# Moving two thirds of the transposes of g from TensorE to the DMA engines in a fused RWKV and MoE kernel

## The chip, the cores and the metric

The kernel runs on one core of a Trainium2 chip. The metric is device time in microseconds (us) of one execution; the time of the kernel before is the median of three runs. A profile is one further execution, taken by the hardware profiler. Engines are written as the profile writes them: PE is TensorE's matmul stream and PEld its weight loads, DVE is VectorE, ACT is ScalarE, POOL is GpSimd, SP is the engine whose queue issues all DMAs of this kernel.

## The reference

Three stages follow each other; what is computed is this (setup and loops cut):

```python
# 1. RWKV recurrence, B=4, H=8, S=768, D=48
cur = einsum('bhd,bhe->bhde', u * k_t, v_t)
y_t = einsum('bhd,bhde->bhe', r_t, state + cur)
state = w_t[..., None] * state + einsum('bhd,bhe->bhde', k_t, v_t)
# x = y as 3072 tokens x 384
# 2. dense MLP, d_ff = 2048
h = x @ w_in;  g = h * cos(h);  x = g @ w_out
# 3. soft MoE, 8 experts x 4 slots, F = 1024
logits = x @ phi
d = softmax over tokens;  slot_input = d.T @ x
slot_out[e] = relu(slot_input[e] @ w1[e]) @ w2[e]
out = softmax over slots(logits) @ slot_out
```

## The kernel before

Tokens are worked in 24 blocks of 128 (index j in the attention, t in the MLP). The 2048 columns of h and g of one block are four **banks** of 512 columns, so there are 24 x 4 = 96 banks; a step is written `name.t.q`, with t the block and q the bank. The order of all steps up to the end of the MLP is a list written out by hand, `HEAD` (line 874 on): each engine gets its instructions in the order in which they stand in it, and waits where an operand is not there. SP's DMAs stand in the same list and run in that order.

One block of the attention is: four loads (`lw`, `lk`, `lr`, `lv`, line 119) and four small ones (`lz`, line 128), transposes on PE (`wT`, `rT`, `kT` at line 136, `kN` at 204), two scans on DVE (`scan` line 151, `sp` line 159, each with two SBUF inputs), two products on POOL (`ru`, lines 164 and 165), an affine select on POOL (`D`, line 211), matmuls `A`, `U` and `y`, and DVE work around them (`L`, `ks`, `mask`, `z`, `st`, `bo`). Its result becomes x as two parts, high and low.

One bank of the MLP is: nine matmuls of 512 columns (`h`, lines 430 to 432); ACT turns it into a number of turns (`turns`, 445), DVE takes the rest (`rest`, 449), ACT the cosine (`cos`, 453), DVE multiplies by h (`mul`, 457). This is g, 128 tokens x 512 columns, in SBUF. The logits need g with its columns on the partitions. So PE transposes the bank in four instructions into PSUM (`gT`, line 464), ACT copies it to SBUF (`gc`, line 470; DVE does seven of the last banks), and four matmuls add it to the logits (`l`, line 479). Two blocks make a group; after its eight banks come the soft-max steps of the group (`sum`, `lc`, `max`, `exp`, `xt`, `xr`, `xd`, `dT`, `dc`, `ltok`) and `E`, which adds g to the slots' sums (line 575, followed by `es` on DVE). The copies of g transposed live in the pool `gt`, 16 - NGB = 3 buffers; g itself has NGB = 13.

After the list stands the end part: the slots' sums go through `w_out` (line 742), the experts' first weights (`hidden`, 761), the second (`expert_out`, 801), and the outputs (`outputs`, lines 832 to 842), which write 24 tiles of 128 tokens in columns 0 to 255 and then in columns 256 to 383. The experts' weights are 16 loads of 1.5 MB (`load_e`, 642 and 646). Six start where the list has `att`, when the attention's buffers are given back, five at the steps `we` of the list, three after the list (`late`), the rest as `hidden` gives buffers back.

Of the kernel before, what the change touches and what calls it, by code (L numbers as in the profile page):

```python
# [21 lines left out]
def rwkv_moe_kernel(ctx: ExitStack, tc: tile.TileContext, r, k, v, w, u, w_in, w_out, phi, w1, w2, cst, out):  # L22
# [592 lines left out]
    if True:  # L615
# [49 lines left out]
        step = {"cs": lambda: nc.sync.dma_start(cs, cst), "neg": lambda: nc.scalar.mul(neg, ident, -1.0), "tab": exp_table, "quart": lambda g: s_quarters(g, lcp[g]), "esl": lambda g, hf: s_e(g, slice(hf * 256, hf * 256 + 256)),
# [17 lines left out]
        late_b = ctx.enter_context(tc.tile_pool(name="late_b", bufs=NLATE - 1, side="right", reuse_waits="tile"))  # L683
# [3 lines left out]
        for i in range(NLATE):  # L687
            load_e(NTW + 5 + i, late_a if i == 0 else late_b, "late")
# [34 lines left out]
        with tc.manual_schedule(engines=ORDERED):  # L723
# [136 lines left out]
            for n0 in range(5, 9):  # L860
                outputs(0, n0)
            for e in range(4, NE):
                expert_out(1, e)
            nc.vector.tensor_copy(so[:, parts[1]], ops[1][:, 0:128])
            for n0 in range(9, 12):
                outputs(0, n0)
# [144 lines left out]
```

## Time and profile before

| | |
|---|---|
| median of 3 runs | 506.11 us (505.91 to 506.32) |
| the profiled execution | 505.58 us |
| its span, first to last instruction | 503.9 us |
| mean granted TensorE clock | 0.993 |
| busy: PE, PEld, DVE, ACT, POOL | 470.7, 369.3, 420.2, 329.6, 101.9 us |

The span is 1.7 us shorter than the profiled execution; what lies around it is no instruction of the program. "Busy" is the union of an engine's instructions in time. Matmuls are pipelined: one begins before the one before it has ended, so what one of them takes from PE is the distance between starts, not its own duration.

### The profile page before, as it was taken

How to read it: one execution, taken by the hardware profiler on the slowest of the kernel's cores; microseconds unless marked ns; L12 is line 12 of the kernel's file. 1: busy time of each engine (PE TensorE's matmuls, PEld its weight loads, DVE VectorE, ACT ScalarE, POOL GpSimd, SP SyncE). 2: the span in 40 equal slices, each digit the busy share in tenths (PEclk: the TensorE clock that was granted, in tenths of full speed). 3: DMA queues.
4: the chain of work that ended last, by engine and by line, in shares of the span. 5: the costliest groups of instructions: out<-in, count | busy, mean ns of one | idle time of the engine just before them, and what ended most of it. 6: DMA issues, size and time to landing. Idle time of an engine off the chain costs nothing.

```text
span 503.9 us, 15604 instructions
## 1 busy us (share of the span) xinstructions
PE 470.7 (93%) x6521; PEld 369.3 (73%) x6521; DVE 420.2 (83%) x820; ACT 329.6 (65%) x724; POOL 101.9 (20%) x127
## 2 busy tenths in 40 slices
PE   2778999999999999999999999999999999997993
PEld 1556788887877878778877778787787887765573
DVE  3999999988999999989889999898889885665423
ACT  5698998876568476765666677666577565573321
POOL 2521223421223312321012303142211000002300
PEclk9999999999999999999999999999999999999997
DMA  9999677524151608423353142263211971398949
GB/s 220 307 259 240 142 206 163 101 50 81 35 92 27 103 2 124 67 43 62 57 89 56 23 75 48 50 95 64 49 22 27 407 277 57 110 404 305 398 138 276
DMA packets 145157, 67.47 MB, mean 134 GB/s; under 512 B 127168, under 2 KB 133568, under 8 KB 145088
## 3 DMA queue, kind: packets, MB, share of 16 engines
q1 hardware_dynamic: 145088, 66.49, 52.9%
q8 instruction: 51, 0.84, 0.7%
q14 instruction: 18, 0.15, 0.1%
HBM read 61.75 MB, written 4.72 MB: 132 GB/s over the span
## 4 chain that ended last, share of the span: by engine, by line
PE 66%; DVE 21%; ACT 6%; DMA 3%; issue 2%; SPq 0%; DVEq 0%; ACTq 0%
PE h L430 10%; PE h L432 9%; PE h L431 9%; PE gT L464 7%; PE l L479 4%; PE y L276 4%; PE E L575 3%; DVE lt L223 3%; DVE g L449 3%; DVE g L457 2%; PE A L197 2%; PE hps L761 2%; PE so L801 2%; DVE pt L159 2%; PE U L248 2%
## 5 line engine op out<-in xcount | busy, mean ns | idle before, releaser
L430 PE MATMUL h<-wu,x 128*128 128x512 f32 (+1 forms) x288 | 118.2, 411 | 1.0 <-DVE g L457 0.7
L432 PE MATMUL h<-wu,x 128*128 128x512 f32 (+1 forms) x288 | 112.7, 391 | 0.0
L431 PE MATMUL h<-wu,x 128*128 128x512 f32 (+1 forms) x288 | 112.4, 390 | 0.0
L453 ACT ACTIVATE g<-g,half_pi 128x512 f32<-128x512 f32 x97 | 69.4, 719 | 37.0 <-DVE g L449 36.3
L445 ACT ACTIVATE g<-h 128x512 int32<-128x512 f32 x96 | 56.9, 595 | 45.1 <-PE h L432 40.6
L457 DVE TENSOR_TENSOR g<-g,h 128x512 f32<-128x512 f32 x96 | 64.9, 679 | 13.2 <-ACT g L453 12.1
L449 DVE SCALAR_TENSOR_TENSOR g<-g,h 128x512 f32<-128x512 int32 (+1 forms) x96 | 64.6, 677 | 9.6 <-ACT g L445 8.6
L430 PEld LDWEIGHTS h<-wu,x 128*128 128x128 f32 x288 | 54.2, 188 | 15.0 <-DVE g L457 4.0
L211 POOL TENSOR_SCALAR_AFFINE_SELECT lt<-bo 64x512 f32<-64x512 f32 x48 | 36.6, 763 | 140.9 <-ACT bo L239 71.5
L432 PEld LDWEIGHTS h<-wu,x 128*128 128x128 f32 x288 | 54.1, 188 | 11.9
L431 PEld LDWEIGHTS h<-wu,x 128*128 128x128 f32 x288 | 54.3, 188 | 9.3
L470 ACT COPY gt<-gT 128x512 f32<-128x512 f32 x89 | 52.1, 585 | 13.1 <-PE gT L464 9.9
L464 PE MATMUL gT<-cs,g 128*128 128x128 f32 x384 | 58.9, 278 | 0.4 <-issue 0.4
L164 POOL TENSOR_TENSOR ru<-rn,u_b 128x384 f32<-128x384 f32 x24 | 25.8, 1074 | 145.4 <-DMA rn<-in_r_dram 72.6
L464 PEld LDWEIGHTS gT<-cs,g 128*128 128x128 f32 x384 | 43.8, 141 | 8.9 <-issue 3.0
L262 ACT COPY rzs<-z 64x192 f32<-64x192 f32 x96 | 33.5, 349 | 1.8 <-DVE z L257 1.0
L180 DVE TENSOR_TENSOR lt<-rT,pt 64x512 f32<-64x512 f32 x48 | 32.8, 684 | 1.8 <-PE rT L136 0.6
L223 DVE COPY_PREDICATED lt<-cs,A 64x256 f32<-64x256 uint32 x72 | 32.2, 447 | 2.2 <-PE A L197 0.7
L479 PE MATMUL l<-gt,p_sb 128*32 128x128 f32 x768 | 31.9, 276 | 0.3 <-DVE gt L470 0.3
L151 DVE TENSOR_TENSOR_SCAN qt<-wf,one_b 128x520 f32<-128x520 f32 x24 | 31.1, 1296 | 0.6 <-ACT wf L146 0.5
L159 DVE TENSOR_TENSOR_SCAN pt<-wf,ini_f 128x520 f32<-128x520 f32 x24 | 31.1, 1295 | 0.1
L165 POOL TENSOR_TENSOR ru<-ru,kn 128x384 f32<-128x384 f32 x24 | 29.8, 1240 | 3.1 <-PE y L276 1.3
(168 smaller groups left out, 770.4 us busy)
## 6 DMA issues: line engine op xcount, KB each, us to landing
we<-in_moe_w_dram SPq DMA_DIRECT2D x16, 1536.0 KB, 10.2
rawo<-in_moe_w_out_dram SPq DMA_DIRECT2D x8, 768.0 KB, 5.5
wn<-in_w_dram SPq DMA_DIRECT2D x24, 192.0 KB, 4.4
kn<-in_k_dram SPq DMA_DIRECT2D x24, 192.0 KB, 3.8
rn<-in_r_dram SPq DMA_DIRECT2D x24, 192.0 KB, 4.0
vn<-in_v_dram SPq DMA_DIRECT2D x24, 192.0 KB, 4.0
rzs<-in_v_dram SPq DMA_DIRECT2D x96, 48.0 KB, 2.8
out_dram<-ob SPq DMA_DIRECT2D x17, 256.0 KB, 3.9
```

Source lines behind the costliest of these rows:

```text
L159: nc.vector.tensor_tensor_scan(pt, wf[:, 0:NS * SEG], ini_f, 0.0, ALU.mult, ALU.add)
L223: nc.vector.copy_predicated(out=lt[j % 2][h, a, c::2], mask=mask[h].bitcast(U32).unsqueeze(1).to_broadcast([64, HP, C]), data=ps[a][o, 0:HP])
L430: nc.tensor.matmul(half[:, f], lhsT=xh[:, c, :], rhs=wh, start=(c == 0), stop=False)
L431: nc.tensor.matmul(half[:, f], lhsT=xl[:, c, :], rhs=wh, start=False, stop=False)
L432: nc.tensor.matmul(half[:, f], lhsT=xh[:, c, :], rhs=wl, start=False, stop=(c == KD - 1))
L445: nc.scalar.activation(gt.bitcast(I32), hp, AF.Copy, bias=0.25, scale=1.0 / TWO_PI)
L449: nc.vector.scalar_tensor_tensor(out=gt, in0=gt.bitcast(I32), scalar=-TWO_PI, in1=hp, op0=ALU.mult, op1=ALU.add)
L453: nc.scalar.activation(gt, gt, AF.Sin, bias=half_pi[:, 0:1])
L457: nc.vector.tensor_tensor(out=gt, in0=gt, in1=hp, op=ALU.mult)
L464: nc.tensor.transpose(ps[:, m * 128:(m + 1) * 128], gt[:, m * 128:(m + 1) * 128], ident)
L470: (nc.vector.tensor_copy if n >= ATT and n % 8 in (1, 2, 5) else nc.scalar.copy)(gt_t[t, q], pend.pop(("gT", t, q)))
L479: nc.tensor.matmul(lps_t[g][32 * m:32 * m + 32, o:o + TB], lhsT=p_sb[:, 4 * q + m, :], rhs=gt[:, m * 128:(m + 1) * 128], start=first, stop ...
```

## The change

In 64 of the 96 banks (numbers 12 to 75, so blocks 3 to 18) the two steps `gT` and `gc` are replaced by three. `gz` copies g, read as pairs of 16-bit numbers, into two planes, one of the first and one of the second halves of each number; bank n goes to ACT where n is a multiple of 3 and to POOL else ("app"), which makes 22 and 42 copies. `gd` stores the planes to device memory as 256 rows of 512 numbers of 16 bits (256 KB). `gx` reads them back with a DMA that transposes, into a buffer that the matmuls `l` read as before. `gd` and `gx` are on SP's queue. Planes and transposed banks have four buffers each, in a new pool `xb` that takes its place where the decoding of the weights has ended (step `close`).

```diff
+    GX = range(12, 76)
+    GSPLIT = "app"
+    NZG = 4
+    NGX = 4
+    def b_gz(t, q):
+        zg = xb_p[0].tile([128, 2, 512], U16, tag="zg", name=f"zg{t}_{q}", bufs=NZG)
+        e = GSPLIT[(NBK * t + q) % len(GSPLIT)]
+        copy = {"a": nc.scalar.copy, "p": nc.gpsimd.tensor_copy, "d": nc.vector.tensor_copy}[e]
+        copy(zg, g_t[t, q].bitcast(U16).rearrange("p (f i) -> p i f", i=2))
+        zg_t[t, q] = zg
+
+    def b_gd(t, q):
+        gs_t[t, q] = gs_p.tile([256, 512], U16, tag="gs", name=f"gs{t}_{q}")
+        nc.sync.dma_start(gs_t[t, q].rearrange("(t i) f -> t (i f)", i=2), zg_t.pop((t, q)).rearrange("p i f -> p (i f)"))
+
+    def b_gx(t, q):
+        gt_t[t, q] = xb_p[0].tile([128, 512], F32, tag="gx", name=f"gx{t}_{q}", bufs=NGX)
+        nc.sync.dma_start_transpose(out=gt_t[t, q].bitcast(U16).rearrange("p (m x) -> p m x", m=4), in_=gs_t.pop((t, q)))
```

The list `HEAD` is new from its first line on. It has the same steps but for these: 64 `gT` and 64 `gc` are gone; 64 each of `gz`, `gd`, `gx` and one `late0` are new. `late0` gives the pool of transposed banks back and starts one of the three late weight loads inside the list, near its end.

In the end part, the outputs are arranged anew: the first 20 tiles are written in columns 0 to 255 without the second half of `expert_out` between them, then in columns 256 to 383, and the last 4 tiles are written once over all 384 columns. Two copies are moved behind `expert_out(0, 1)`, and one small DVE instruction stands one place earlier.

```diff
+        def early_late():
+            t_stack.close()
+            load_e(NTW + 5, ctx.enter_context(tc.tile_pool(name="late0", bufs=1, reuse_waits="tile")), "late")
...
-            if c.start == 0:
+            if c.start == (256 if g == NG - 1 else 0):
...
+            def rows(k):
+                if "r" not in obs:
+                    obs["r"] = wu_p.tile([128, NTT // 2 - NA // 2, 2, DM], F32, tag="wu3", name="obr")
+                ob = obs["r"][:, k - NA // 2]
+                for i in range(2):
+                    ps = pb(f"r{k}_{i}")[:, 0:DM]
+                    nc.tensor.matmul(ps, lhsT=crf[:, 256 * k + i:256 * k + 256:2], rhs=sr, start=True, stop=True)
+                    (nc.scalar.copy if i else nc.vector.tensor_copy)(ob[:, i], ps)
+                nc.sync.dma_start(out[256 * k:256 * k + 256, :].rearrange("(p i) f -> p (i f)", i=2), ob.rearrange("p i f -> p (i f)"))
...
-            for n0 in range(2, 5):
+            for n0 in range(2, NA // 2):
                 outputs(0, n0)
-            for e in range(1, 4):
+            for e in range(1, NE):
                 expert_out(1, e)
...
-            for n0 in range(6):
+            for n0 in range(NA // 4):
                 outputs(1, n0)
+            for k in range(NA // 2, NTT // 2):
+                rows(k)
```

## Rows read from the trace of the kernel before

**Rows 1.** Page, part 2: PE and its clock, in 40 slices of the span
```profile
PE   2778999999999999999999999999999999997993
PEclk9999999999999999999999999999999999999997
```
**Rows 2.** Windows: busy time of each engine, granted clock, DMA share, GB/s
```profile
core 0: us, PE busy (x) PEld busy (x) DVE busy (x) ACT busy (x) POOL busy (x), PEclk, DMA share, GB/s
0.00:100.00 100.00, 82.25 (x1113) 64.64 (x1114) 89.21 (x128) 83.53 (x168) 30.62 (x47) 1.00 0.89 206
100.00:400.00 300.00, 296.25 (x4287) 236.94 (x4289) 275.04 (x562) 197.15 (x447) 64.65 (x71) 1.00 0.37 69
400.00:450.00 50.00, 49.73 (x466) 38.45 (x458) 34.97 (x78) 30.68 (x64) 0.00 (x0) 1.00 0.55 211
```
**Rows 3.** Waits of PE between 100 and 400 us: total, times, longest
```profile
PE h L430 <- DVE g L457: 0.7, 2, 0.6
PE E L575 <- DVE ltok L562: 0.7, 1, 0.7
```
**Rows 4.** Timeline of PE, 240 to 250 us: start, duration, line
```profile
241.13 0.60 PE L464 MATMUL gT<-cs,g 128*128 128x128 f32 x4
241.66 0.68 PE L248 MATMUL U<-vn,ksn 64*64 64x48 f32 x32
...
246.25 0.66 PE L464 MATMUL gT<-cs,g 128*128 128x128 f32 x4
246.67 0.47 PE L430 MATMUL h<-wu,x 128*128 128x512 f32 x1
```
**Rows 5.** Groups by line: count, busy us, mean ns of one, idle before
```profile
L470 ACT COPY gt<-gT 128x512 f32<-128x512 f32 x89 | 52.1, 585 | 13.1 <-PE gT L464 9.9 <-PE l L479 2.9
L361 ACT CAST wu<-ai 128x768 fp32r<-128x768 f32 x8 | 6.7, 841 | 1.3 <-DVE ai L348 1.1
L721 POOL CAST cr<-cr 32x384 fp32r<-32x384 f32 x8 | 3.8, 500 | 6.5 <-issue 4.7 <-ACT cr L719 1.5
L165 POOL TENSOR_TENSOR ru<-ru,kn 128x384 f32<-128x384 f32 x24 | 29.8, 1240 | 3.1 <-PE y L276 1.3
L164 POOL TENSOR_TENSOR ru<-rn,u_b 128x384 f32<-128x384 f32 x24 | 25.8, 1074 | 145.4 <-DMA rn<-in_r_dram 72.6 <-DVE bo L234 45.1 <-DVE g L457 24.9
```
**Rows 6.** One line each: duration ns minimum, median, maximum
```profile
L211 POOL TENSOR_SCALAR_AFFINE_SELECT lt<-bo x48: 651/656/1781, 21.5 to 384.6; 64x512 f32<-64x512 f32 x48
L165 POOL TENSOR_TENSOR ru<-ru,kn x24: 1001/1022/1919, 15.0 to 357.6; 128x384 f32<-128x384 f32 x24
L151 DVE TENSOR_TENSOR_SCAN qt<-wf,one_b x24: 1226/1234/2047, 11.8 to 378.2; 128x520 f32<-128x520 f32 x24
L128 SPq DMA_DIRECT2D rzs<-in_v_dram x96: 595/614/2719, 18.6 to 378.0; - x96
```
**Rows 7.** Timeline of DVE and of POOL around 357 us
```profile
356.57 2.05 DVE L151 TENSOR_TENSOR_SCAN qt<-wf,one_b 128x520 f32<-128x520 f32 x1
356.32 1.20 POOL L164 TENSOR_TENSOR ru<-rn,u_b 128x384 f32<-128x384 f32 x1 [4.92 <-DMA rn<-in_r_dram]
357.59 1.83 POOL L165 TENSOR_TENSOR ru<-ru,kn 128x384 f32<-128x384 f32 x1
```
**Rows 8.** DMA issues: KB each, median us from issue to landing
```profile
we<-in_moe_w_dram SPq DMA_DIRECT2D x16, 1536.0 KB, 10.2
rn<-in_r_dram SPq DMA_DIRECT2D x24, 192.0 KB, 4.0
out_dram<-ob SPq DMA_DIRECT2D x17, 256.0 KB, 3.9
```
**Rows 9.** Windows of the end part, columns as in the windows above
```profile
485.00:490.00 5.00, 5.00 (x81) 4.34 (x83) 2.89 (x6) 2.62 (x7) 0.00 (x0) 1.00 0.60 196
490.00:495.00 5.00, 4.89 (x87) 4.50 (x80) 2.76 (x6) 1.80 (x5) 0.00 (x0) 1.00 0.94 310
495.00:500.00 5.00, 1.22 (x11) 1.07 (x10) 1.54 (x3) 1.08 (x2) 0.00 (x0) 0.67 1.03 305
```
**Rows 10.** Timeline of DVE at the end: its last instruction
```profile
496.25 0.69 DVE L841 COPY ob<-o 128x512 f32<-128x512 f32 x1 [0.20 <-PE o L834]
```

More of the change, by code (lines that the diff above doesn't have):

```diff
@@ L862, in rwkv_moe_kernel @@
[L862 to L866, printed above, removed]
+            nc.scalar.copy(so[:, parts[1]], ops[1][:, 0:128])
             slots_out(1)
             slots_round(1)
-            for n0 in range(6):
+            slots_rest(1)
+            for n0 in range(NA // 4):
                 outputs(1, n0)
+            for k in range(NA // 2, NTT // 2):
+                rows(k)
@@ L939 @@
-turns.15.3 h.16.1 gc.15.0 mask.19 rT.20 wT.21 lr.21 sr.20 rest.15.3 gT.15.2 turns.16.1 lk.21 y.18 es.6 ru.21 l.15.0 cos.15.3 xh.18 D.20 mul.15.3
-l.15.1 h.16.0 rz.19.1 lr.22 sp.20 rest.16.1 gc.15.2 xl.18 bo.21 cos.16.1 wf.21 turns.16.0 kN.20 gT.15.3 ksn.20 mul.16.1 y.19 l.14.3 L.20 l.15.2
-scan.21 lw.23 rest.16.0 lw.22 gc.15.3 sr.21 l.15.3 rz.20.0 sum.7 U.20 gT.16.1 lk.22 xh.19 cos.16.0 st.20.0 lc.7 ru.22 max.7 exp.7 h.16.2 mul.16.0
-gc.16.1 h.16.3 z.20.1 turns.16.2 st.20.1 xl.19 rz.20.1 xt.7 xr.7 rest.16.2 cos.16.2 turns.16.3 xd.7 A.20 mul.16.2 rest.16.3 cos.16.3 sp.21 kT.21
@@ new lines @@
+lk.6 om.2 rest.1.2 cos.1.2 wT.6 mul.1.3 xm.3 lk.5 pc.2 lr.6 mask.4 rz.4.0 lr.5 h.2.1 gc.0.3 xc.3 d2b.o.7 pT.2 lz.4 sr.5 gT.1.1 ps.2 ru.5 abs.o.6 oT.14
+mul.1.2 rz.4.1 oT.15 h.2.0 gc.1.1 z.6.0 d2a.o.6 oc.15 kT.5 oc.14 sp.5 lw.8 wf.6 d2b.o.6 close gT.1.0 lw.7 ks.5 l.0.2 turns.2.0 bo.5 rT.5 gc.1.0 lr.7
+oT.13 oc.13 z.5.0 oT.12 ru.6 rest.2.0 cos.2.0 gT.1.2 l.1.0 l.1.1 y.4 oc.12 L.5 xh.4 bs.5 gc.1.2 D.5 om.3 rT.6 xm.4 kN.5 turns.2.1 mul.2.0 scan.6 sr.6
+xc.4 pc.3 bo.6 gT.1.3 lk.7 h.2.2 sp.6 pT.3 ksn.5 gc.1.3 rest.2.1 gT.2.0 bs.6 L.6 l.1.2 ps.3 l.1.3 l.0.3 U.5 turns.2.2 rest.2.2 A.5 cos.2.1 sum.0
@@ new lines @@
+rest.10.3 l.9.2 sp.15 l.9.3 xh.13 gd.10.0 sum.4 U.14 lc.4 xl.13 gz.10.2 st.14.0 cos.10.3 max.4 z.14.1 D.14 mul.10.3 h.11.1 exp.4 xt.4 A.14 turns.11.1
+lv.16 st.14.1 xr.4 rest.11.1 xd.4 mask.14 lz.14 h.11.0 cos.11.1 dT.4 ltok.4 gz.10.3 lr.16 gd.10.2 rz.14.1 mul.11.1 z.15.0 dc.4 kT.15 wT.16 rz.14.0
+gx.10.0 bo.15 E.4.0 rT.15 turns.11.0 wf.16 ks.15 rest.11.0 lv.15 cos.11.0 scan.16 lk.17 gx.10.1 h.11.3 mul.11.0 kN.15 l.10.0 bs.15 lk.16 turns.11.3
+lr.17 rest.11.3 sr.16 ksn.15 E.4.1 L.15 U.15 cos.11.3 h.11.2 l.10.1 y.14 lw.18 D.15 st.15.0 gz.11.0 rz.15.0 mul.11.3 ru.17 sp.16 gz.11.1 z.15.1
@@ new lines @@
+gd.11.0 gx.10.2 turns.11.2 rest.11.2 xh.14 cos.11.2 h.12.2 gd.11.1 kT.16 gz.11.3 es.4 xl.14 turns.12.2 st.15.1 mul.11.2 bo.17 gd.10.3 rest.12.2
+cos.12.2 A.15 gz.11.2 gx.11.0 ks.16 gd.11.3 ru.16 gd.11.2 mask.15 h.12.0 mul.12.2 wT.17 turns.12.0 gx.10.3 l.10.2 wf.17 gx.11.1 rest.12.0 l.11.0 rT.16
+bo.16 gx.11.2 h.12.1 cos.12.0 rz.15.1 turns.12.1 kN.16 gx.11.3 scan.17 mul.12.0 z.16.0 ksn.16 l.10.3 h.12.3 rest.12.1 cos.12.1 sr.17 lv.17 L.16
+rz.16.0 wT.18 bs.16 l.11.1 l.11.2 l.11.3 turns.12.3 gz.12.2 bs.17 sp.17 sum.5 rest.12.3 mul.12.1 wf.18 U.16 lc.5 cos.12.3 kT.17 h.13.0 st.16.0 max.5
@@ new lines @@
+lw.20 z.17.1 gd.13.1 gx.12.1 L.18 gz.13.2 cmb.1.2 kT.18 l.12.1 turns.14.0 wf.19 gd.13.0 l.12.2 rest.14.0 cos.14.0 st.17.1 l.12.3 A.17 mul.13.3 h.14.1
+gz.13.3 scan.19 ks.18 ru.19 mul.14.0 lz.17 gd.13.2 gx.13.0 gd.13.3 sr.19 turns.14.1 mask.17 rz.17.1 rest.14.1 wT.20 kN.18 cos.14.1 bo.19 gz.14.0
+h.14.3 gx.13.1 gx.13.2 l.13.0 lr.20 cmb.1.4 ksn.18 gx.13.3 turns.14.3 mul.14.1 gd.14.0 l.13.1 U.18 h.14.2 sp.19 l.13.2 rest.14.3 l.13.3 st.18.0 lk.20
+cmb.1.3 rz.18.0 lw.21 wf.20 cos.14.3 lv.20 bs.19 turns.14.2 A.18 lv.19 sum.6 mul.14.3 rest.14.2 gz.14.1 es.5 h.15.1 cos.14.2 turns.15.1 mask.18
@@ new lines @@
+gz.17.2 cos.19.1 gx.17.0 es.7 l.16.3 kN.22 gd.17.2 gx.17.1 h.18.1 wf.23 ksn.22 turns.18.1 mul.19.1 z.22.0 U.22 D.22 gx.17.3 scan.23 rest.18.0 l.17.0
+st.22.0 z.22.1 rest.18.1 st.22.1 y.21 gx.17.2 l.17.1 lr.23 xh.21 cos.18.0 cos.18.1 h.19.2 l.17.2 l.17.3 sr.23 sum.8 rz.22.1 xl.21 A.22 sp.23 mul.18.1
+mul.18.0 lc.8 mask.22 h.18.3 lz.22 max.8 gz.18.0 exp.8 kT.23 xt.8 h.18.2 turns.19.2 xr.8 turns.18.3 gz.18.1 xd.8 rz.22.0 rest.18.3 ks.23 gd.18.1
+rest.19.2 dT.8 gx.18.1 ru.23 dc.8 h.19.3 rT.23 cos.18.3 cos.19.2 ltok.8 mul.18.3 E.8.0 turns.18.2 mul.19.2 gz.18.3 L.23 kN.23 ksn.23 h.19.0 z.23.0
```

226 lines of the change are left out of this document (110 added, 116 removed).

## The prediction

> **What bounds the kernel now.** I read the 40 slices first, then the busy time by stage, then PE's waits, and only then single instructions. PE is full from the fourth slice to the last but three, at the full clock, 1.00 or 2.4 GHz [rows 1, 2]. The clock drops only after the matmuls have ended (0.67 in the window from 495 us [rows 9]), so nothing here turns on it. Three stages differ. Until 100 us no engine is full: DVE has 89.2 us, ACT 83.5, PE 82.3. From 100 to 400 us PE has 296.3 of 300 us, DVE 275.0, ACT 197.2, POOL 64.7, and the DMA engines a share of 0.37. From 400 to 450 us PE has 49.7 of 50 and DVE only 35.0 [rows 2]. In the middle stage PE's longest waits for another engine add up to 0.7 us per cause [rows 3]. So PE is the bound there, with DVE 21 us behind it. Blocks 3 to 18 of the 24, where the change works, fill most of that middle stage.
>
> **What is removed.** A bank's four transposes take from PE the distance from their first start to the start of what follows: 241.66 - 241.13 = 0.53 us in one place, 246.67 - 246.25 = 0.42 in another [rows 4]. I take the middle, 0.48 us. For 64 banks that is 64 x 0.48 = 31 us (27 to 34). PE's need in the middle stage falls from 296.3 to about 265.5 us. ACT loses 64 copies of 585 ns [rows 5], 37 us.
>
> DVE loses nothing: the seven copies that it makes belong to later banks, and `rest`, `mul` and the attention stay. So DVE, with its 275.0 us, becomes the longest queue of the stage, and the 31 us can't all come off. 300 - 275.0 = 25 us is the most that the stage can give, while DVE's work stays there.
>
> **What is added, on the engines.** ACT gets 22 copies of 1024 elements. The rows give 585 ns for 512 and 841 for 768 [rows 5], 1.0 ns per further element, so 1.1 us each, 24 us in all; ACT ends at 197 - 37 + 24 = 184 of some 288 us and is no bound. POOL gets 42 copies of 1024 elements. No row shows one. With one input it does 384 elements in 500 ns [rows 5] and 512 in 656 [rows 6], 1.22 ns per further element, so 1.3 us; with two inputs it takes 1022 ns for 384 [rows 6], 2.7 ns per element, so 2.7 us at the worst. I take 1.3, since the copy has one input: 42 x 1.3 = 55 us (to 113). POOL goes from 65 to 120 us (at most 178) of the stage.
>
> POOL's reading is not free for DVE, though. A scan takes 1234 ns in the median and up to 2047 [rows 6]; the long one, 2.05 us, lies beside POOL's product of 356.32 to 357.52, and the next product, which should take 1.02, takes 1.83 beside that scan [rows 7]. One waits for the other. The mean of the scan of line 151 is 1296 ns by the page's group, 62 above its median; 24 x 0.062 = 1.5 us, and as much for the other scan, 3 us for 55.6 us of products [rows 5]. POOL's copies, 55 us of reading, should cost DVE as much again, 3 us, and 1 for the short products with two SBUF inputs: 4 us. Bounds: nothing, if they fall between the scans; 9, if the copies last 2.7 us.
>
> **What is added, on the queues.** SP gets 128 more DMAs. The bulk of those issued now hold it for 0.61 us (the 96 small ones of `lz` [rows 6]); 128 x 0.61 = 78 us, on a queue that issues some eight DMAs per block now. It is not full. But it is in order: a `gx` waits for the landing of its own `gd`, and the next blocks' loads are queued behind it, as are the other banks' stores. Who waits for those loads first is POOL's `ru` (72.6 us of idle before it is for `rn` [rows 5], harmless today) and then DVE's `bo`. I price this at nothing, because the list puts other issues between `gd` and `gx`; if that cover fails, it is the landing rival below.
>
> The DMA engines get 64 stores and 64 reads of 256 KB. Big loads ran at 1536 KB in 10.2 us from issue to landing [rows 8], 0.15 MB per us with the latency in it; the attention's loads moved 69 GB/s at a share of 0.37 [rows 2], which is 186 GB/s when busy, so 1.4 us per 256 KB. The outputs moved at 305 to 310 GB/s [rows 9], 0.85 us. For a store I take 0.85, for a transposing read, of which there is no row, 1.4; the stage's share becomes (0.37 x 300 + 64 x 2.25) / 288 = 0.89. That is much, and it is hidden as long as it stays under 1. The Trainium skill ("DMA: Bandwidth & Descriptors", Latency and other measured facts) gives a transposing DMA 261 GB/s where the middle dimension is not contiguous; 256 KB would then be an estimated 1.0 us, and the share 0.80. No run here shows it.
>
> **The sum.** The middle stage becomes DVE's 275.0, plus 4 for POOL, plus the time in which DVE waits. PE, when it was the bound, was idle 3.75 us in 300. DVE stands behind two engines in every bank (`turns` and `cos` on ACT), and a bank's logits now hang on two DMA landings, so I take 9. 275 + 4 + 9 = 288, 12 less than 300.
>
> In the end part the last copy ends at 496.94 us [rows 10], and the span at 503.9: 7.0 us in which only output DMAs run. They move 196 GB/s from 485 to 490 us and 305 to 310 after it [rows 9]. With 20 tiles issued in one go the first 5 us could run at the later rate: 5 x (310 - 196) / 310 = 1.8 us. I take 2; bounds 4 (wider rows at the end help too) and -1 (the queue runs dry while the second half of `expert_out` is computed). The early weight load and the small moves I price at nothing: no wait of the end part in the trace is for weights. If a gap in the weight loads opens, it costs at most one load, 10.2 us [rows 8]. The stages before 100 and from 400 to 450 us keep their work; the list orders them anew, which I can't price and put at nothing.
>
> So 12 + 2 = 14 us off the profiled 505.6, 491.6; off the median of the runs, which is 0.5 above the profiled one, 492.0.
>
> **The rivals.**
> *DVE packs as tightly as PE did.* Idle 3.75, no collisions, 4 at the end: 300 - 278.8 + 4 = 25 off, 481. For it: DVE has other blocks' work ready most of the time. Against: the collisions are in the trace already [rows 7].
>
> *The landings come too late.* Today a bank is ready for `l` one copy (0.6 us) after its transposes. Then it is a copy (1.1 to 1.3), a store's landing, and a read's landing, each near the 3.9 to 4.0 us of the nearest rows [rows 8], some 9 us. Counted in the new list, 1 to 7 steps `h` of other banks (median 4) stand between a bank's `gz` and its `l`; before, 0 to several (median 2) stood between `gT` and `l`. If a tight bank in each block waits 1 us, PE's spare 22 us absorb it. If every group's last banks wait 2 to 3 us on PE, and DVE then waits for the next `h`, 8 groups x 1.5 us = 12 us, which is the whole gain of the middle stage; only the 2 us of the end are left, 504.
>
> *Transposing reads are slow, and the DMA engines become the bound; this is the slower side.* Left for them are 288 - 111 (today's) - 54 (stores) = 123 us, 1.9 us per bank. Above that point the stage lengthens by 64 us for each further us. At twice the attention's price, 2.8 us, the stage is 111 + 54 + 179 = 344, 44 more than now: 505.6 + 44 - 2 = 548. For it: 16-bit pieces are smaller than any piece the kernel moves now, and smaller ones ran at 186 against 310 GB/s. Against: no row shows the transposing path at all. A table of the Trainium skill speaks for this rival ("VectorE: DVE Perf Modes", The three transpose paths): 128x128 numbers of 16 bits take 1309 ns by DMA against 390 by TensorE; eight such squares per bank would be an estimated 10.5 us if they didn't overlap. Another page says the opposite ("Advanced Engine Details and Errata", X-Bar Transpose (TRN2)): such DMAs are as fast as others. No run here tells.
>
> **How the numbers follow.** Forecast 486 to 500: 0.62. Tight packing: 0.10, 480 to 486. Late landings: 0.14, 500 to 506 by how many groups wait, most of it still a gain of more than 0.2% (1 us, about what a measurement of this kernel can tell from no change). Slow reads: 0.12, from 507 to 550. Waits in orders that I can't see leave 0.02 beyond. The range 481 to 504 leaves out the slow reads, a third of the late landings and a little of the tight case. Faster: 0.62 + 0.10 + 0.10 = 0.82; the same 0.04; slower 0.14.
>
> **What would show it.** In the middle stage PE should fall to about 92% busy and DVE rise to 95% or more; PE's waits should name DVE (`mul`, `mask`), not a landing of `gx`. If DVE stays near 92% and PE's waits name `l` behind a DMA, it was the landings; if the DMA share is 1 through the stage, the reads. POOL's copies should take 1.3 us, and the scans' mean rise above 1296 ns. At the end the output rate should be near 310 GB/s from the first 5 us. The forecast is wrong if DVE's work left the stage, or if the list shortens the first 100 us.

## The result, and the profile after

The changed kernel takes 500.54 us in the median of four runs (497.82 to 504.26), against 506.22 us (505.91 to 506.89) for the kernel before beside it: a ratio of 0.9886, 95% interval 0.9855 to 0.9917. The gain is 5.7 us; 14 were forecast. 500.5 us lies inside the stated range, but in the stretch that the prediction gave to late landings (500 to 506, 0.14), not in its forecast of 486 to 500. The profiled execution took 500.44 us, its span 498.7. By the last `mul` of block 19 the changed kernel is 3.7 us ahead (393.5 against 397.2 us from the start), by the end of the list 3.9, at the end 5.2. So most of what was to come off the middle stage didn't.

The page's strips, beside [rows 1]: a digit is a fortieth of the span.
```profile
PE   1678999999999899997999998998999999998993
PEclk9999999999999999998999999999999999999998
DMA  9999978346989969999498899988995579789938
```
The windows of the stages, with the columns of [rows 2], which they answer:
```profile
0.00:100.00 100.00, 81.74 (x1114) 63.99 (x1115) 89.40 (x128) 83.88 (x166) 30.52 (x49) 1.00 0.88 203
100.00:400.00 300.00, 283.84 (x4056) 211.93 (x4055) 279.24 (x566) 191.33 (x412) 107.97 (x111) 0.99 0.89 169
400.00:450.00 50.00, 48.96 (x468) 37.17 (x470) 34.70 (x80) 30.69 (x63) 0.00 (x0) 1.00 0.88 337
125.00:375.00 250.00, 234.48 (x3355) 174.39 (x3354) 232.24 (x467) 155.45 (x332) 95.40 (x97) 0.99 0.96 181
```
In the middle stage no engine is full now: PE 95%, DVE 93%, and the DMA share has gone from 0.37 to 0.89, to 0.96 where the change is at work throughout (the last line). PE has holes that [rows 1] don't have, and its clock has one. PE's waits from 100 to 400 us (total, times, longest) beside [rows 3] name a new cause:
```profile
PE l L503 <- DMA gx<-gs: 7.4, 8, 2.9
PE h L437 <- DVE g L464: 1.6, 3, 1.0
```
The new operations, by line: duration in ns minimum, median, maximum.
```profile
L485 POOL COPY zg<-g x42: 1029/1042/1926, 118.9 to 392.4; 128x1024 uint16<-128x1024 uint16 x42
L485 ACT COPY zg<-g x22: 1029/1046/1057, 117.1 to 387.2; 128x1024 uint16<-128x1024 uint16 x22
L494 SPq DMA_TRANSPOSE gx<-gs x64: 1226/1292/3645, 124.3 to 395.5; - x64
L490 SPq DMA_DIRECT2D gs<-zg x64: 332/524/2352, 120.0 to 393.5; - x64
```
And in the list of issues, with median us from issue to landing:
```profile
gs<-zg SPq DMA_DIRECT2D x64, 256.0 KB, 3.3
gx<-gs SPq DMA_TRANSPOSE x64, 4.1
```
A transposing read holds SP's queue for 1.29 us in the median, twice the 0.61 us of [rows 6]. From 125 to 375 us the issues add up to 201 of 250 us: 59 reads 88, 57 stores 34, 58 small loads of `rz` 40, 57 other loads 39. Before, it was 80. An SP that isn't issuing here mostly stands at a wait, in order.

One place shows what that does. SP's timeline (start, duration, instruction):
```profile
215.48 1.88 SPq L494 DMA_TRANSPOSE gx<-gs  x1
217.42 0.57 SPq L126 DMA_DIRECT2D wn<-in_w_dram  x1
218.09 0.53 SPq L490 DMA_DIRECT2D gs<-zg  x1
218.71 1.24 SPq L126 DMA_DIRECT2D wn<-in_w_dram  x1
220.00 2.60 SPq L135 DMA_DIRECT2D rzs<-in_v_dram  x4
222.69 0.55 SPq L126 DMA_DIRECT2D rn<-in_r_dram  x1
223.34 1.51 SPq L490 DMA_DIRECT2D gs<-zg  x3
224.91 5.61 SPq L494 DMA_TRANSPOSE gx<-gs  x3
```
The timelines of POOL and of PE, their first work after a wait:
```profile
226.12 1.02 POOL L171 TENSOR_TENSOR ru<-rn,u_b 128x384 f32<-128x384 f32 x1 [6.19 <-DMA rn<-in_r_dram]
230.92 0.42 PE L503 MATMUL l<-gx,p_sb 128*32 128x128 f32 x8 [2.93 <-DMA gx<-gs]
```
And windows of 2 us around it, columns as above:
```profile
226.00:228.00 2.00, 1.99 (x83) 1.36 (x81) 1.93 (x5) 1.36 (x4) 1.80 (x2) 1.00 1.38 329
228.00:230.00 2.00, 0.00 (x0) 0.00 (x0) 2.00 (x6) 1.96 (x4) 1.33 (x2) 1.00 1.53 138
230.00:232.00 2.00, 1.08 (x11) 0.79 (x12) 2.00 (x5) 0.03 (x1) 0.00 (x0) 1.00 0.83 182
232.00:234.00 2.00, 2.00 (x7) 1.57 (x6) 0.16 (x1) 0.00 (x0) 1.04 (x1) 0.55 1.05 324
234.00:236.00 2.00, 2.00 (x10) 1.57 (x9) 0.58 (x1) 1.21 (x3) 0.00 (x0) 0.60 0.58 129
```
SP issues from 215 to 230.5 us with hardly a gap. The load of `rn`, for which POOL has stood 6.2 us, gets its turn at 222.69; the read for which PE will wait, at 224.91. That read lands 6.0 us after its issue (the median is 4.1), while the packets of two windows add up to 1.38 and 1.53 of the time that 16 DMA engines have. PE is idle 2.93 us. Some 1.3 us after it has resumed, the granted clock falls to half (1.2 GHz) for some 3.4 us: another 1.7 us. So this hole costs 4.6 us of PE, and two things make it: the place of the read in SP's queue, and a landing 1.8 us longer than the median.

### The profile page after: what moved, and what is told of

Same layout as the page of the kernel before. It is cut to its first block, busy times and chain, and to the rows that moved or that the text cites. A ratio compares the mean times of both kernels' runs of the same rounds, so it can differ in the third digit from the quotient of the medians.

```text
span 498.7 us, 15329 instructions
## 1 busy us (share of the span) xinstructions
PE 453.5 (91%) x6261; PEld 340.1 (68%) x6261; DVE 421.5 (85%) x819; ACT 322.2 (65%) x684; POOL 145.2 (29%) x169
## 4 chain that ended last, share of the span: by engine, by line
PE 56%; DVE 14%; DMA 11%; ACT 6%; issue 5%; SPq 4%; POOL 2%; ACTq 0%; POOLq 0%; DVEq 0%
PE h L437 9%; PE h L439 8%; PE h L438 8%; DMA gx<-gs 7%; PE l L503 3%; PE E L599 3%; PE gT L471 3%; DMA rn<-in_r_dram 2%; PE y L283 2%; PE hps L790 2%; PE so L827 2%; PE A L204 2%; DVE pt L166 2%; PE U L255 2%; DVE g L456 2%
## 5 line engine op out<-in xcount | busy, mean ns | idle before, releaser
L437 PE MATMUL h<-wu,x 128*128 128x512 f32 (+1 forms) x288 | 122.3, 425 | 1.6 <-DVE g L464 1.6
L439 PE MATMUL h<-wu,x 128*128 128x512 f32 (+1 forms) x288 | 113.6, 395 | 0.0
L438 PE MATMUL h<-wu,x 128*128 128x512 f32 (+1 forms) x288 | 113.1, 393 | 0.0
L460 ACT ACTIVATE g<-g,half_pi 128x512 f32<-128x512 f32 (+1 forms) x97 | 69.4, 719 | 37.8 <-DVE g L456 37.0
L452 ACT ACTIVATE g<-h 128x512 int32<-128x512 f32 (+1 forms) x96 | 57.0, 596 | 53.3 <-PE h L439 43.2
L485 POOL COPY zg<-g 128x1024 uint16<-128x1024 uint16 x42 | 46.6, 1112 | 117.3 <-DVE g L464 72.1
L464 DVE TENSOR_TENSOR g<-g,h 128x512 f32<-128x512 f32 (+1 forms) x96 | 64.3, 675 | 4.6 <-ACT g L460 3.9
L166 DVE TENSOR_TENSOR_SCAN pt<-wf,ini_f 128x520 f32<-128x520 f32 x24 | 32.8, 1367 | 0.1
L503 PE MATMUL l<-gx,p_sb 128*32 128x128 f32 x512 | 23.4, 280 | 7.6 <-DMA gx<-gs 7.4
L172 POOL TENSOR_TENSOR ru<-ru,kn 128x384 f32<-128x384 f32 x24 | 27.9, 1163 | 4.5 <-DMA kn<-in_k_dram 2.7
L283 PEld LDWEIGHTS y<-lt,rzs 128*32 128x32 f32 x1536 | 23.9, 110 | 6.6 <-issue 5.3
L599 PE MATMUL E<-g,dt 128*32 128x512 f32 (+1 forms) x208 | 25.2, 567 | 2.4 <-ACT dt L580 1.6
```

The source lines that it names most:

```text
L166: nc.vector.tensor_tensor_scan(pt, wf[:, 0:NS * SEG], ini_f, 0.0, ALU.mult, ALU.add)
L437: nc.tensor.matmul(half[:, f], lhsT=xh[:, c, :], rhs=wh, start=(c == 0), stop=False)
L438: nc.tensor.matmul(half[:, f], lhsT=xl[:, c, :], rhs=wh, start=False, stop=False)
L439: nc.tensor.matmul(half[:, f], lhsT=xh[:, c, :], rhs=wl, start=False, stop=(c == KD - 1))
L452: nc.scalar.activation(gt.bitcast(I32), hp, AF.Copy, bias=0.25, scale=1.0 / TWO_PI)
L460: nc.scalar.activation(gt, gt, AF.Sin, bias=half_pi[:, 0:1])
```

## The experiments

The expectations name theories by letters. L: the 16 DMA engines are too full. Q: SP's queue is too long, and what stands in it comes late. S: the list leaves too little time for one bank's chain of copy, store and read. V: DVE can't be packed tighter.

All numbers of the runs, each with its own kernel before beside it (506.1 to 506.8 us); "share" (of the 16 DMA engines), "SP" (the sum of the issues that start there, us) and "PE on gx" (us of PE's waits for a landing of `gx`) are of 125 to 375 us; "clock" is the PE time lost to a lower clock from 100 to 400 us, the sum over windows of 10 us of what the granted clock lacks of 1.00.

| run | us | ratio, 95% | share | SP | PE on gx | clock |
|---|---|---|---|---|---|---|
| before | 506.2 | | 0.36 | 80 | - | 0 |
| after | 500.5 | 0.986-0.992 | 0.96 | 201 | 7.4 | 1.7 |
| e1_no_dma | 493.8 | 0.973-0.979 | 0.34 | 77 | - | 0 |
| e2_l_reads_g | 501.1 | 0.987-0.992 | 0.96 | 205 | - | 5.1 |
| e3_half_read | 491.9 | 0.969-0.974 | 0.74 | 191 | 0.3 | 1.7 |
| e4_end_part | 506.1 | 0.996-1.001 | 0.36 | 81 | - | 0 |
| e5_tiny | 505.3 | 0.995-0.999 | 0.69 | 211 | 10.3 | 3.4 |
| e11_tiny_act | 495.8 | 0.977-0.982 | 0.70 | 193 | 0.6 | 1.7 |
| e8_plain_read | 491.4 | 0.968-0.972 | 0.73 | 138 | 0 | 0 |
| e10_small_packets | 491.4 | 0.969-0.974 | 0.85 | 163 | 0.9 | 0 |
| e14_small_both | 508.4 | 0.999-1.005 | 0.90 | 200 | 11.9 | 5.1 |
| e13_half_rz | 496.3 | 0.975-0.983 | 0.93 | 182 | 5.4 | 1.7 |
| e15_lw_act | 496.2 | 0.973-0.981 | 0.98 | 193 | 5.1 | 0 |
| e17_lw_lk_act | 505.5 | 0.995-0.999 | 0.95 | 172 | 5.8 | 6.8 |
| e18_lw_lk_lr_act | 507.2 | 0.998-1.002 | 0.95 | 164 | 10.2 | 8.6 |
| e9_store_act | 510.8 | 1.006-1.012 | 0.93 | 172 | 14.0 | 6.8 |
| e6_three_quarters | 496.1 | 0.976-0.981 | 0.78 | 172 | 0 | 0 |
| e16_three_quarters_lw | 495.9 | 0.976-0.980 | 0.79 | 163 | 0 | 0 |
| e12_three_quarters_act | 506.1 | 0.998-1.001 | 0.80 | 150 | 5.7 | 0 |
| e7_half | 512.2 | 1.006-1.014 | 0.61 | 127 | 0 | 5.1 |

The last two columns say where the time is lost. The profiled run of e8 took 491.1 us; with the two columns added to it, the profiled runs of the changed kernel, e3, e5, e9, e10, e13, e14, e15, e17 and e18 come out within 1.4 us (changed kernel: 491.1 + 7.4 + 1.7 = 500.2, measured 500.4; e9: 511.9, measured 513.3). The sum is 3.5 us short in e11 and 6.1 in e2, where PE waits for no read; the runs with fewer banks have more work on PE and aren't counted.

**Where the gain goes: the DMAs, not the engines.** e1 takes the 64 stores and reads out, and `l` reads g as it is:
```diff
-HEAD: gd, gx
+        gt = g_t[t, q] if NBK * t + q in GX else gt
```


> The changed kernel without its 64 stores and 64 transposing reads; the 16-bit copies stay, and the logits' matmuls read g itself, not transposed (so the logits are other numbers; the instructions of PE, DVE, ACT and POOL are the same). Theory L (the DMA engines are too full: share 0.96 between 125 and 375 us, landings late): the waits go, and DVE's work sets the pace, 488 to 492 us. Rival S (the list leaves too little time for the chain of copy, store and read, whatever the load): also 488 to 492. Rival V (DVE can't be packed tighter than it is): stays at 497 to 501.

493.8 us, near the 488 to 492 of theories L and S and above them by 1.8. Its windows:
```profile
100.00:400.00 300.00, 290.02 (x4190) 218.15 (x4189) 286.75 (x579) 196.20 (x422) 109.92 (x111) 1.00 0.39 81
```
Without the DMAs, DVE is at 286.75 of 300 us and the last `mul` of block 19 ends 11.7 us earlier than before. The copies on POOL and ACT don't hold the gain back; something about the DMAs does.

e2 keeps every DMA, and only lets `l` read g itself, so that nothing of the kernel waits for a landing of `gx`:
```diff
+        gt = g_t[t, q] if NBK * t + q in GX else gt
```


> All stores and transposing reads stay, but the logits' matmuls of these 64 banks read g itself, so no matmul waits for a transposing read (the logits are other numbers). Rival S: as without any DMA, 488 to 492 us. Theory L: the attention's loads still come late and SP's queue is as long, so only part of it comes back: 493 to 497. Rival V: 497 to 501.

501.1 us, no gain over the changed kernel, where L had 493 to 497. It is V's range, but V is out by e1. So the chain of copy, store and read before each `l` isn't all of the price: with that wait gone, others take its place, and the clock loses 5.1 us for 1.7. POOL's waits of this run and PE's two first, 125 to 375 us:
```profile
POOL ru L171 <- DMA kn<-in_k_dram: 11.1, 1, 11.1
POOL ru L171 <- DMA rn<-in_r_dram: 9.6, 4, 5.2
POOL zg L485 <- DMA wn<-in_w_dram: 6.6, 1, 6.6
PE h L437 <- DVE g L464: 4.6, 6, 2.5
PE kT L143 <- DMA kn<-in_k_dram: 3.3, 1, 3.3
```
The attention's loads come late, although nobody waits for a read. POOL's wait for `rn` alone is no sign of a loss: before, it was 35.4 us here, and harmless. But PE now stands 3.3 us for a load of k.

e3 reads back only half of each bank (128 KB), and `l` reads that half twice:
```diff
-        dma_start_transpose(out=gt_t[t, q] ... m=4), in_=gs_t.pop((t, q)))
+        dma_start_transpose(out=gt_t[t, q][:, 0:256] ... m=2), in_=gs_t.pop((t, q))[:, 0:256])
```


> Each transposing read fetches half of the columns (128 KB in place of 256), and the logits' matmuls read that half twice; number of DMAs, stores, copies and waits as in the changed kernel (the logits are other numbers). Theory L: DMA work of the stage falls by 56 us of 16 engines (half of 64 x 1.75), its share from 0.9 to 0.7; 493 to 496 us. Rival S: a landing is shorter by under 1 us, so 498 to 500. Rival V: 500.

491.9 us. The middle stage now gives 11.8 us to the end of block 19. At this point I read these three runs as "the DMA engines are too full": the share fell from 0.96 to 0.74. The next runs took that reading away; e3 alone can't give it, because SP's issues fell too (201 to 191 us) and each read landed sooner (3.3 us in the median for 4.1).

**The end part alone.** e4 is the list of before with `late0` behind `l.23.3`, and the new end part.

> The list of the kernel before (all transposes on PE) with the new end part and the early late load, which stands behind the last matmul of the logits. My prediction put the end part at 2 us: 504.2. By the two traces the end of the list came 3.9 us earlier and the span got 5.2 us shorter, so 1.3 us: 504.9. Rival: the end part is worth nothing by itself, 506.2.

506.1 us, ratio 0.9962 to 1.0005. From the end of the list to the end of the span it takes 43.6 us, as the changed kernel does, against 44.9 before; but the list ended 1.8 us later in its profile, and the times show no gain. The interval reaches 1.9 us down, so 1.3 us aren't excluded.

**SP's queue against the DMA engines.** e5 is e3 with a copy of 16 bytes behind each read, on SP's queue; e11 is the same with those copies issued by ScalarE.
```diff
+        ty = xb_p[0].tile([1, 4], F32, tag="ty", name=f"ty{t}_{q}", bufs=4)
+        nc.sync.dma_start(ty, cst[0:1, 0:4])        # e11: nc.scalar
```


> The run with half the transposing read, with one more thing: behind each of the 64 reads, SP issues a copy of 16 bytes to a tile that nobody reads. It adds some 0.5 us of SP's queue for each, 32 us in all, and next to no bytes: SP's issues then take about 223 us of the stretch 125 to 375, more than the changed kernel's 201, at a DMA share that stays near 0.74. As in the run without the tiny copies, half of each bank's transposed copy is left out. Theory L (the 16 DMA engines are too full, SP's queue doesn't matter): 491 to 494 us. Rival Q (the cost is SP's queue, on which the attention loads stand behind the stores and reads): 497 to 502 us.

> The run with half the read and 64 tiny copies, with the tiny copies issued from ScalarE's queue in place of SP's. As there, half of each bank's transposed copy is left out. Theory Q: back to the 492 us without them (491 to 494), plus at most 1 us for ScalarE's issues. If the tiny copies cost by what they do at the DMA engines, wherever they are issued: 500 to 506 us.

505.3 us, 3 above what Q gave, and 495.8 us. The tiny copies hold SP 0.43 us each (e5, by line):
```profile
L496 SPq DMA_DIRECT2D ty<-in_const_dram x63: 413/428/452, 125.3 to 396.0; - x63
```
And PE's waits for `gx` are back, at a share of 0.69 (e5, waits of 125 to 375 us):
```profile
PE l L505 <- DMA gx<-gs: 10.3, 9, 3.5
```
13.4 us for 27 us of queue and no bytes; 9.5 of them go when another queue issues the same copies. That shows that more issues in SP's queue cost, with DMA engines that are far from full; whether by the time they hold SP or by their place behind each read isn't told apart. The 3.9 us that e11 stands above e3 are more than the 1 us that I allowed for ScalarE.

e8 reads back the whole 256 KB per bank with a plain DMA (both planes then hold the upper halves, and `l` multiplies an untransposed bank). e10 is e8 with the read cut into packets of 256 bytes; e14 cuts the stores as well.
```diff
-        nc.sync.dma_start_transpose(out=gt_t[t, q] ...)
+        nc.sync.dma_start(gt_t[t, q].bitcast(U16), gs_t.pop((t, q)).rearrange("(t i) f -> t (i f)", i=2))
```


> All stores stay, and each bank is read back whole (256 KB), but by a plain copy in place of the transposing one, with packets of 2048 bytes in place of 256; what the table matmul then multiplies isn't the transposed bank, and both planes hold the upper halves. By the store's own packets (128 of 96 ns, 0.77 us of 16 engines) the read falls from 1.75 to 0.77 us per bank, so the DMA share of 125 to 375 goes from 0.96 to about 0.71. Theory L, with the transposing read's slow packets as what fills the engines: 491 to 494 us, as with half the read. If the bytes count, whatever their packets: 499 to 502 us.

> The run with a plain read, with its 256 KB per bank cut into 1024 packets of 256 bytes in place of 128 of 2048; again what the table matmul multiplies isn't the transposed bank. At 21 to 27 ns a packet the read takes 1.3 to 1.75 us of 16 engines per bank, and the DMA share of 125 to 375 rises from 0.73 to 0.88 to 0.97, at SP's issues near that run's 138 us. Theory Q: as with the large packets, 490 to 494 us. Theory L: 498 to 502 us.

> The run with a plain read in packets of 256 bytes (491.4 us, share 0.85), with the stores cut the same way: 1024 packets of 256 bytes in place of 128 of 2048. At 19 ns a packet a store takes 1.2 us of 16 engines in place of 0.77, and the DMA share of 125 to 375 comes to about 0.96, that of the changed kernel, with SP's issues at some 165 to 175 us in place of its 201. What the table matmul multiplies isn't the transposed bank. Theory Q: 490 to 494 us. Theory L: 498 to 502 us.

491.4, 491.4 and 508.4 us. The windows of e8, and behind it of e10:
```profile
125.00:375.00 250.00, 241.56 (x3455) 180.90 (x3444) 240.81 (x488) 162.46 (x349) 100.33 (x100) 1.00 0.73 186
```
```profile
125.00:375.00 250.00, 241.36 (x3437) 180.58 (x3438) 240.29 (x487) 161.71 (x349) 99.05 (x100) 1.00 0.85 186
```
How long an issue holds SP, the read in e10, then read and store in e14:
```profile
L494 SPq DMA_DIRECT2D gx<-gs x64: 518/553/2425, 124.4 to 386.8; - x64
```
```profile
L494 SPq DMA_DIRECT2D gx<-gs x62: 517/756/2275, 125.7 to 393.5; - x62
L490 SPq DMA_DIRECT2D gs<-zg x63: 513/836/2513, 120.9 to 397.0; - x63
```
e10 has a share 0.12 above e8's and the same time, so here, up to 0.85, the load of the DMA engines costs nothing. e14 was to tell the two causes apart at 0.96 and doesn't: with small stores, too, each issue holds SP longer (0.84 us for a store, 0.76 for a read), SP comes to 200 us instead of the 165 to 175 I expected, the share to 0.90, and its time lies above what either theory gave (490 to 494, 498 to 502). No transposing read is in it, and PE waits 11.9 us for `gx`. It has the SP sum of the changed kernel and is 8 us slower, so that sum alone doesn't order the times.

**Relief for SP, with the transposing reads as they are.** e13 leaves out the loads of `rz` for 8 of the blocks 8 to 23, whose `y` takes the values of two blocks before. e15 leaves nothing out; it lets ScalarE issue the loads of w from block 8 on.
```diff
+        if j >= 8 and j % 4 >= 2: return                     # e13, in load_rz
-            nc.sync.dma_start(dst[j % 2] ...)
+            (nc.scalar if src is w and j >= 8 else nc.sync).dma_start(dst[j % 2] ...)   # e15
```


> The changed kernel, where the four loads of rz are left out for 8 of the blocks from 8 to 23 (10, 11, 14, 15, 18, 19, 22, 23), whose y then reads the values of two blocks before: 32 issues of some 0.6 us and what SP waits for y ahead of them are gone from SP's queue, and 8 x 1.15 = 9 us of the 16 DMA engines' time, which leaves the DMA share of 125 to 375 at about 0.93. Theory Q (SP's queue): 494 to 497 us, about half or more of the lost 8 us back. Theory L (DMA share): 499 to 500 us.

> The changed kernel, where the loads of w from block 8 on (16) are issued from ScalarE's queue, which by then has itself waited for the transpose that frees their buffer. Nothing is left out. SP loses 16 x 0.6 = 10 us of issues and the waits ahead of them. Theory Q: 495 to 499 us. Theory L: 500 to 502 us.

496.3 and 496.2 us. The window of e15, and PE's first wait in it:
```profile
125.00:375.00 250.00, 237.88 (x3484) 176.67 (x3477) 236.07 (x476) 158.00 (x339) 97.03 (x99) 1.00 0.98 184
```
```profile
PE l L503 <- DMA gx<-gs: 5.1, 8, 1.5
```
The DMA engines are fuller than in the changed kernel (0.98), and the kernel is 4.4 us faster (e14, at 0.90, is 12 us slower than e15): a full DMA share alone doesn't set the 500 us, and a shorter queue on SP (193 for 201 us) gives back about half of what is lost. The longest wait for `gx` is 1.5 us instead of 2.9, and the clock stays at 1.00.

e17 lets ScalarE issue the loads of k as well, e18 those of r too (the condition reads `src is w or src is k`, then `src is not v`).

> The changed kernel, where the loads of w and of k from block 8 on (32) are issued from ScalarE's queue. Nothing is left out. SP's issues of 125 to 375 fall to about 183 us, the DMA share stays at 0.98. Theory Q: 491 to 494.5 us. If the rest lies with the DMA engines: 495.5 to 497 us. If ScalarE now stands waiting for the buffers of k with its own work behind: above 498 us.

> As the run before it, with the loads of r from block 8 on there too (48 in all). Nothing is left out. SP's issues of 125 to 375 fall to about 174 us. Theory Q: 490.5 to 493.5 us. If the rest lies with the DMA engines: 495.5 to 497 us. If ScalarE now stands waiting for buffers with its own work behind: above 498 us.

505.5 and 507.2 us: worse, with SP at 172 and 164 us, and in the range that the expectations gave to a ScalarE that has to wait (above 498). In e17 one load of k can be followed to PE. ScalarE issues it at 167.18; the timelines of ScalarE, POOL, DVE and PE (the first work after a wait), and the windows in which the clock fell:
```profile
167.18 0.37 ACTq L126 DMA_DIRECT2D kn<-in_k_dram  x1
172.04 0.99 POOL L172 TENSOR_TENSOR ru<-ru,kn 128x384 f32<-128x384 f32 x1 [3.84 <-DMA kn<-in_k_dram]
173.07 0.55 DVE L241 TENSOR_REDUCE bo<-ru 128x8 f32<-128x384 f32 x1 [3.32 <-POOL ru L172]
174.07 1.13 PE L204 MATMUL A<-lt,ks 64*64 64x64 f32 x30 [3.18 <-DVE st_state L272]
```
```profile
170.00:180.00 10.00, 6.28 (x92) 4.29 (x85) 6.85 (x14) 4.59 (x8) 5.25 (x6) 0.65 0.88 119
180.00:190.00 10.00, 10.00 (x104) 7.81 (x102) 7.08 (x20) 5.33 (x14) 1.06 (x1) 0.84 0.38 112
```
ScalarE issues a load at its place among ScalarE's own work. The buffer of w is freed by a transpose that ScalarE has itself waited for by then; that of k, by PE's `kT` and POOL's `ru`. Here a late `kn` costs PE 3.2 us and the clock 5.1 more. That this is so in e18 too, and that it is all of the loss, isn't shown.

e9 has ScalarE issue the 64 stores (`nc.scalar.dma_start` in `b_gd`).

> The changed kernel with one edit: the 64 stores are issued from ScalarE's queue in place of SP's. Nothing is left out, and no byte is saved, so the DMA share of 125 to 375 should stay near 0.96; SP's issues fall by 64 x 0.52 = 33 us of the list, to about 170 of these 250 us; ScalarE, busy 191 of the 300 us from 100 to 400, gets them. Theory Q (SP's queue, on which the attention loads stand behind stores and transposing reads, costs the lost 8 us): 491 to 495 us. Theory L (the 16 DMA engines are too full): 499 to 502 us.

510.8 us, slower than before and outside what both theories gave (491 to 495, 499 to 502), though SP's issues fell to 172 us as expected. SP's first wait, 125 to 375 us:
```profile
SPq L494 <- DMA gs<-zg: 54.0, 22, 5.3
```
The stores are issued late, among ScalarE's work, and SP stands in front of the reads until they land: 54 us, against 10.2 in the changed kernel. What SP no longer issues it now waits, and the loads stand behind it all the same.

**Fewer banks by DMA.** e6 puts every fourth bank back on PE (48 by DMA), e7 every second (32); e12 is e6 with the stores on ScalarE, e16 e6 with the loads of w there.

> 48 of the 64 banks stay on the DMA way, 16 (every fourth) go back to TensorE with ScalarE's copy. The DMA share of 125 to 375 should fall from 0.96 to about 0.39 + 0.75 x 0.57 = 0.82; TensorE gets 16 x 0.48 = 8 us more and still stands under VectorE. Theory L: most of the lost gain comes back, 493 to 496 us. A theory by which the gain goes with the number of banks moved (each bank by DMA is worth 5.7/64 us): 506.2 - 0.75 x 5.7 = 502 us.

> 32 of the 64 banks stay on the DMA way, 32 (every second) go back to TensorE with ScalarE's copy. DMA share of 125 to 375 about 0.39 + 0.5 x 0.57 = 0.67; TensorE is 15 us fuller than in the changed kernel, and again about as full as VectorE. Theory L: 494 to 498 us, with TensorE and VectorE sharing the bound. Gain by the number of banks: 503 us.

> 48 banks by DMA as in the run with three quarters (496.1 us), with their stores issued from ScalarE's queue. Nothing is left out. SP's issues fall from 172 to about 145 of the stretch 125 to 375. Theory Q: 491 to 495 us, and faster than the 496.1 by 1 to 4. Theory L (DMA share 0.78 is not too full, so the rest lies elsewhere): 495 to 497 us.

> 48 banks by DMA as in the run with three quarters (496.1 us), and the loads of w from block 8 on from ScalarE's queue. Nothing is left out. Theory Q: SP's issues fall from 172 to about 163 of the stretch 125 to 375, and 492 to 495 us. Theory L: 496 to 497 us.

496.1, 512.2, 506.1 and 495.9 us. e6 and e16 leave nothing out and beat both kernels: 16 banks fewer by DMA, 4.5 to 4.6 us faster than with all 64. In e6 PE doesn't wait for `gx` at all, and e16's further relief of SP gives nothing more, so there it isn't SP that is left. e12 repeats e9, 9 us above its expectations: SP waits 75.4 us for stores to land. e7 went against every theory. Its PE waits for none of the reads; its first wait from 100 to 400 us is
```profile
PE gT L471 <- ACT gt L477: 7.3, 6, 2.7
```
and SP waits 64 us for planes (100 to 400 us). I placed the `gT` and `gc` of these banks in the list by a rule; whether that order is the loss wasn't tried, and e7 settles nothing on the DMAs.

## Why the prediction was wrong

**The step that failed** is the price of SP's queue: 128 more DMAs "on a queue that issues some eight DMAs per block now", "priced at nothing, because the list puts other issues between `gd` and `gx`". That looked at one bank's store and read. Two things were off. The size: 0.61 us for each [rows 6], 78 us in all; it was 0.58 on average for a store, but 1.49 for a read, so 133 us. And the cover: I let the queue be hidden as long as it wasn't full, though I wrote that it is in order. At 201 of 250 us in issues it has little left for its waits, and a late issue moves what is behind it. In place of nothing the runs show about half of the 8.6 to 9.1 us by which the changed kernel stands above e3, e8 and e10, or more: e5 and e11 show that more issues on SP cost at a share of 0.69, and e15 that 4.4 us come back when SP's issues fall by 8 us.

**What stays open** is the other half, from 496.2 (e15) to 491.4 (e8). e13 and e15 have shares of 0.93 and 0.98 and PE still waits 5 us for `gx`; landings take 4.3 us in e15, 3.3 in e3. That may be the DMA engines, or the queue. At nearly the same sum on SP (193 and 191) e15 stands 4.3 us above e3, with a share of 0.98 for 0.74, which speaks for the engines; e11, at 0.70 and 193, stands at 495.8, which doesn't. e14 was to tell and couldn't; e17 and e18 brought a new cost. The intervals of e15 and e8 nearly touch (0.973 and 0.972).

**The DMA engines.** The share came out as forecast, 0.89 in 100 to 400 us, in part by luck: two sizes were off in opposite directions, and the stage was longer. A store was smaller (0.77 us of 16 engines for 0.85) and the transposing read larger: 1024 packets of 256 bytes at 27 ns are 1.75 us for my 1.4, under the 1.9 at which the slow-read rival decides. That rival (548 us) is out. Its argument that these pieces are smaller than any other was wrong too: the attention's packets have 192 bytes. "Hidden as long as it stays under 1" holds at 0.85 (e10); above that it isn't settled. The Trainium skill's 261 GB/s ("DMA: Bandwidth & Descriptors", Latency and other measured facts) gave an estimated 1.0 us; the trace, beside the kernel's other traffic, has 150 GB/s. The Trainium skill also has transposing DMAs as fast as others ("Advanced Engine Details and Errata", X-Bar Transpose (TRN2)). Here they weren't: the read takes 1.75 us of the 16 engines, a plain one 0.80 (e8), or 1.24 in packets of the same size (e10), and it holds SP for 1.29 us where the plain ones hold it for 0.38 and 0.55.

**The rival of late landings** gave 500 to 506 us, and the time is at its low end; PE's eight waits for `gx` are what it named. Its reason was at most part of the right one. It counted the length of one bank's chain and the steps between `gz` and `l`; but with the same chain these waits are 10.3 us in e5 and 0.6 in e11, and e2, without them, takes as long. Landings do have a part. The trace has the landing of seven of the eight reads, and five of them took 4.5 to 6.0 us. At the median of 4.1, PE would have waited an estimated 3.8 us less of its 7.4, worked out from these landings; the other half they don't explain.

**The clock.** "Nothing here turns on it" was wrong: behind a hole of 2.9 us PE ran at half clock for 3.4 us. In the changed kernel that is 1.7 us, in the slower variants up to 8.6.

**What was right.** PE's gain: the start distances of `gT` add up to 15.3 us for 45.9, 30.6 less (31 forecast). The middle stage: 12 us were forecast, and 11.7, 11.8, 13.2 and 12.5 came by the end of block 19 in e1, e3, e8 and e10, where the DMAs don't hold it up. There DVE stands at 95 to 96%, as said. PE stands at 97%, not at 92: matmuls and weight loads stretch into the time that is left, and which of the two engines sets these 491 us no run tells.

**POOL's copies and DVE.** The copies took 1.11 us on POOL for 1.3, 1.04 on ACT for 1.1. For contention with DVE I took 4 us, 3 of them on the scans. The size was about right, but it fell elsewhere, as the groups by line show:
```profile
L166 DVE TENSOR_TENSOR_SCAN pt<-wf,ini_f 128x520 f32<-128x520 f32 x24 | 32.8, 1367 | 0.1
L158 DVE TENSOR_TENSOR_SCAN qt<-wf,one_b 128x520 f32<-128x520 f32 x24 | 30.1, 1253 | 0.6 <-ACT wf L153 0.5
L264 DVE TENSOR_TENSOR z<-st_state,qt 128x192 f32<-128x192 f32 x44 | 20.1, 458 | 0.1
```
Both scans together are 0.7 us more than before, with 46.6 us of copies on POOL, and the six scans that a copy lies beside took 1.23 us, as those beside no work of POOL did. The short product `z` is 3.3 us more than before (16.8 us, 382 ns): beside a copy it took 0.78 us on average, beside no work of POOL 0.34.

**The end part.** I took 2 us; the trace shows 1.3 between list and end, and e4's times none. The step "20 tiles issued in one go run at the later rate" failed: the windows of the end, beside [rows 9], are
```profile
480.00:485.00 5.00, 5.00 (x68) 4.55 (x69) 3.71 (x7) 3.17 (x7) 0.00 (x0) 1.00 0.53 170
485.00:490.00 5.00, 4.62 (x102) 4.35 (x94) 0.97 (x3) 1.31 (x4) 0.00 (x0) 1.00 0.97 319
```
The first 5 us still move 170 GB/s while PE works through the tiles, and from the last copy (491.95) to the end it is 6.8 us as it was 7.0.

## What to carry to other kernels

Price the issuing queue as an engine: so many issues by the time that each holds it, plus its waits, in order; when the sum comes near the stage's length, what stands behind comes late, even with DMA engines that are not full (here 211 of 250 us cost 13.4 us at a share of 0.69, and 191 cost nothing that shows). The Trainium skill names this case ("Perfetto Trace Analysis", What "DMA-bound" means: the sequencer of the issuing engine), and its advice to spread issues over engines (DMA Optimizations) held here for loads whose buffer the other engine has already waited for (e15, 4.4 us) and failed for loads and stores that ScalarE issued late (e9, e12, e17, e18). And offload no more than pays: 48 banks were 4.5 us faster than 64, though 32, in an order that I didn't tune, were 11.6 slower.

## What the runs showed of the hardware that was not expected

- How long an issue holds SP depends on the traffic and on the packets: the same store holds it for 0.34 us in the median beside plain reads (e8), for 0.52 beside transposing ones; a plain read of 256 KB for 0.38 us in packets of 2048 bytes, 0.55 in packets of 256 (e10), 0.76 with small stores beside it (e14). Half the bytes of a transposing read hold it for 1.22 us, hardly less than 1.29 (e3).
- Packets of 256 bytes take 27 ns each in the changed kernel's transposing reads and 19 in plain ones (e10); with three quarters as many transposing ones they took 25 (e6), with half as many some 20 (e3).
- The changed kernel's runs spread over 6.4 us, those of e8 over 1.4. A hole of PE that brings a stretch at half clock costs 1.7 us on top of itself in the changed kernel and up to 5.1 in e17. That this makes the spread isn't shown: the fastest of the four runs (497.82 us) has a mean clock of 0.988, the profiled one 0.993.
